# One explicit table for the order of 1435 operations, in place of a list scheduler, in a one-core attention and feed-forward kernel

## The chip, the core and the metric

The kernel runs on one core of one Trainium2 chip. That core has a matrix engine (TensorE, called PE below), a vector engine (DVE), a scalar engine (ACT), a general engine (POOL) and a synchronising engine (SP). Each runs its own instructions[...] and waits on semaphores for the others. Here POOL and SP mainly issue DMA transfers. The metric is the device time of one execution in microseconds, as the median of several runs, lower being better.

## What is computed

Eight batches of twelve heads go through an attention whose softmax is replaced by a squared ReLU. Its output, a matrix of 3584 rows and 768 columns, goes through a feed-forward block of width 2048 with an exact GELU.

```python
# batch 8, heads 12, sequence S = 448, head width 64
scores = scale * np.matmul(q, k.transpose(0, 1, 3, 2))
attn = np.maximum(scores, 0.0) ** 2 / S
x = np.matmul(attn, v)          # -> (3584, 768)
h = x @ w_in                    # 768 x 2048
g = 0.5 * h * (1.0 + erf(h * inv_sqrt2))
return g @ w_out                # 2048 x 768
```

## The kernel before

The kernel describes its work as 1435 objects of class `Op`. An `Op` is a short burst of work on one engine, such as four matmuls of one score tile, or one copy. It names the engines that may run it with assumed durations, the operations it depends on, and the buffers it takes and frees. A scheduler written in Python decides at build time the order on each engine and, where an `Op` may run on ACT or DVE, which of the two runs it. Nothing of the scheduler runs on the chip; only the order that it made does.

The operations fall into kinds. Letters in brackets are the `mode` of PE operations.

- Score tiles `fn_qk` [A]: four or eight matmuls with stationary tiles of 64 x 64, which use the four quarters of the array side by side, into a buffer `ps` out of three of the PSUM pool `w`. `fn_relu` (ACT or DVE) brings them to SBUF, `fn_mul` (DVE) squares them there.
- `pav` [A]: 28 matmuls of squared scores with values, also on quarters, once seven score tiles are squared. Two copies (ACT or DVE) bring them to `xT`.
- First feed-forward product [F]: `psh` for batches 0 to 4, and `pb` (one level of Strassen's method, with sums formed on DVE) for batches 5 to 7, on the whole array of 128 x 128. ACT applies GELU.
- Second product `pso` [F]: four plain products, then 13 groups of seven Strassen products each, into a buffer out of two of the PSUM pool `f`; copied or added into an output tile `osb`, of which there are three, and stored.
- Transposes on PE [T] for batches 0 and 1, `tp`. For batches 2 to 7 the transposes are done by DMA, issued from SP, and stores are issued from SP as well.
- `fill` [A]: matmuls of zeros early on, to keep PE busy.

```python
SWITCH = 0.09
PASSES = 5
...
ORDER = """
A10 P11 D13 A16 D12 P17 D18 P14 G0 P42 A15 G1 P39 A40 G2 P19 D43 ...   # 267 operations,
... Z1056 P69 ...               # Z: a fill of so many columns
"""
...
    def pick(self, ops, only=None):
        ...
                if eng == "PE" and op.mode != self.mode:
                    est += SWITCH
                key = (est + op.bias + x * op.other, n)
        ...

    def run(self, fixed):
        best = None
        for _ in range(PASSES):
            self.reset()
            self.place(fixed)
            self.deadlines()
            end = self.free["PE"]
            if best is None or end < best[0]:
                best = (end, list(self.log))
        self.open, self.log = [], best[1]

        def at(x):
            est, op, eng = x
            if eng not in ("ACT", "DVE"):
                return est
            return est + next(lat for e, _, lat in op.engines if e == eng)

        for est, op, eng in sorted(self.log, key=at):
            op.fn(eng)

    def place(self, fixed):
        ...
        for word in ORDER.split():          # first the table
            if word[0] == "Z":
                op, eng = next(fills), "PE"
            else:
                op, eng = self.open[int(word[1:])], names[word[0]]
            ...
            self.commit(max(self.ready(op), free), op, eng, dur, lat)
        ...
        while rest or any(fixed.values()):  # then the list scheduler
            ...                             # earliest estimated start first
```

The score tile, its evacuation and its square:

```python
            o1 = sch.add((("PE", d, d + 0.24),), fn_qk, deps, need=("w",), mode="A", bias=bias)
            d = 0.19 + 0.00069 * 2 * used
            eng = (("ACT", d, d + 0.14),)
            d = 0.07 + 2 * used / 960
            if dve:
                eng += (("DVE", d, d + 0.12),)
            o2 = sch.add(
                eng, fn_relu, [o1], need=("a",), frees=("w",), bias=bias, other=RELU_DVE
            )
            ...
            o3 = sch.add((("DVE", d, d + 0.12),), fn_mul, [o2], bias=bias)
```

A group of the second product. `v2` and `v3` take the two output tiles of the group; `p4` needs `v3`, and `p3` needs `c22`:

```python
        p1 = product("a", lambda: h(0, o1), lambda: quad[0, 0], done, need=("f",))
        v1 = passed("a", first, None, [p1], need=("p",))
        p6 = product("b", lambda: box["s", 2], lambda: tsum(2), done + sums + [s2], need=("f",), frees=("s2",))
        ...
        v2 = passed("b", part(0, right), first, [v1, p6], need=("osb",))
        p2 = product("a", lambda: h(1, o1), lambda: quad[1, 0], [v1])
        ...
        p7 = product("b", lambda: box["s", 3], lambda: tsum(3), [v2, s3], frees=("s3",))
        v3 = passed("b", part(1, right), first, [p7], need=("osb",))
        p5 = product("c", lambda: box["s", 1], lambda: tsum(1), [s1, s2], need=("f",), frees=("s1",))
        c22 = passed("c", part(1, right), part(1, right), [v3, p5])
        p4 = product("b", lambda: h(1, o2), lambda: tsum(4), [v3])
        ...
            sch.add((("SP", 0.6, 2.8),), store(1, full, [nc.sync] * 2), [c22, c21], frees=("osb",))
```

The DMA transposes are issued from SP, in the queue in which the stores stand; a small copy on POOL, the `gate`, waits for them and lets the loads of the next batch be issued:

```python
            return sch.add(
                (("SP", T_STEP, T_TIME),),
                lambda e: nc.sync.dma_start_transpose(dst(), src()),
                deps + old_T(b) + after.pop(0), mode="X",
            )
```

Of the kernel before, what the change touches and what calls it, by code (L numbers as in the profile page):

```python
# [47 lines left out]
RELU_DVE = 0.8  # L48
DMA_FREE = 3.05
DMA_LAT = 2.13  # L50
SWITCH = 0.09
LEAD = 8
HALF_M = 6
PASS_BIAS = -0.4
SUM_BIAS = -0.3
# [1 line left out]
LEADS = {}  # L57
SHARES = (1.3, 1.0, 1.0, 1.0, 1.0, 1.0)
LAST = 256
PASSES = 5  # L60
PULL = 0.15
PULL_IN = 0.45
NEAR = 0.25
# [17 lines left out]


ORDER = """
A10 P11 D13 A16 D12 P17 D18 P14 G0 P42 A15 G1 P39 A40 G2 P19 D43 G3 D44 P21 A22 P33 D20 P36 G4
Z128 P54 G5 P25 A37 P23 A55 G6 P51 D34 P48 A24 A49 D26 D35 D56 D41 D38 A52 Z1056 P69 D70 G7
Z1024 P57 Z992 P63 A58 D53 Z448 P45 D50 P66 G8 G9 D59 A64 A46 P27 P31 D28 G117 D32 A67 D65 D68
A47 G118 P60 P78 G119 A61 P29 D30 G120 P81 A79 A82 D62 G121 G122 Z1088 P93 A94 D71 P108 Z544
P84 A85 Z992 P75 D109 A76 D83 D80 P72 P90 D73 P129 D95 P105 A74 G123 P102 A91 D130 A106 P131
D86 D77 G124 D132 P141 D92 A103 P111 P96 G125 A112 P165 P143 A97 D104 P156 D107 A166 A157 P87
D113 D98 P99 D110 D88 G126 A142 D89 P114 P174 P133 D100 G127 A101 A175 D115 D116 P159 A144  # L90
P168 D134 G128 P171 D169 A160 P135 D172 D173 D170 A136 G147 P251 P192 D193 P186 P162 A252 P145
D176 A163 A146 P243 P253 P180 P195 A187 A244 P198 P137 A254 G148 D164 D158 P139 G149 G150 A181
D167 G151 A199 D161 P183 D196 A184 P177 D138 D140 D188 G152 P189 P219 P245 P247 D194 A178 A190
S231 A220 D185 A179 P207 P216 A246 S229 D182 P213 D191 D197 P261 A248 A208 S232 P263 S228 D200
A214 P222 D217 P204 D221 D209 P201 D215 A262 A223 A264 P210 A211 P265 G153 S230 A266 P259 A260
P249 P255 D218 D205 A202 A250 A203 P257 D224 G154 A256 D206 D212 P225 P267 G155 A258
"""


# [14 lines left out]
class Scheduler:  # L114
# [110 lines left out]
        self.open, self.log = [], best[1]  # L225


        def at(x):
            est, op, eng = x
            if eng not in ("ACT", "DVE"):  # L230
                return est
            return est + next(lat for e, _, lat in op.engines if e == eng)

        for est, op, eng in sorted(self.log, key=at):
            op.fn(eng)

    def deadlines(self):
# [97 lines left out]
def kernel(  # L335
# [119 lines left out]
    def e_copy(n, psum=4):  # L455
# [4 lines left out]
    sch = Scheduler({"w": 3, "a": NA, "f": 2, "osb": 3, "s1": 1, "s2": 1, "s3": 1, "s4": 1,  # L460
                     "p": 1})
# [384 lines left out]
    def add_wsums(after, done):  # L846

        last = [o[0] for (bb, *_), o in list(Tq.items()) + list(Tk.items()) if bb == B - 1]
        last += [o for (bb, *_), o in QK.items() if bb == B - 2]
        add, sub = mybir.AluOpType.add, mybir.AluOpType.subtract  # L850

        def one(n, m0, op, a, b, deps):
            m1 = m0 + M1 // 2
            return sch.add(
                (("DVE", 0.95, 1.07),),
                lambda e: V.tensor_tensor(wcols(n, m0, m1), a(m0, m1), b(m0, m1), op=op),
                deps + last + after,
            )

        def part(i, j):  # L860
            return lambda m0, m1: wpart(i, j, m0, m1)

        def summed(n):
            return lambda m0, m1: wcols(n, m0, m1)

        for m0 in (0, M1 // 2):
            s1 = one(1, m0, add, part(0, 1), part(1, 1), [])
            s2 = one(2, m0, sub, summed(1), part(0, 0), [s1])
            s4 = one(4, m0, sub, part(1, 0), summed(2), [s2])
            s3 = one(3, m0, sub, part(0, 0), part(0, 1), [s1] + done)  # L870
            WS[m0] = {1: s1, 2: s2, 3: s3, 4: s4}
# [48 lines left out]
    def add_block(b, m4, y, ms, bank, x, t, TS, xs, old, half):  # L920

        tmp = {}

        def product(name, left, right, deps, first=False):
            def fn(e):
                if first and name not in bank:
                    bank[name] = w_pp.tile([128, 2, NB], F32, tag="w", name="pb")
                for z, m in enumerate(ms):
                    w, mm = left(m)
                    for k in range(K1):  # L930
                        nc.tensor.matmul(  # L931
                            bank[name][:, y, z * HS : z * HS + HS],
                            w[:, k, bass.ts(mm, 128)],
                            right()[:, k],
                            start=first and k == 0 and z == 0,
                            stop=k == K1 - 1,
                            skip_group_check=not first or z > 0,
                        )

            d = 2 * K1 * (HS / 2400 + 0.0025)  # L940
            return sch.add(
                (("PE", d, d + 0.24),), fn, deps, mode="F",
                need=("w",) if first and y == 0 else (),
            )

        def plain(i, j):
            return lambda m: (wpart(i, j), m)

        def summed(n):
            return lambda m: wtile(n, m)  # L950

        def ps(name):
            return bank[name][:, y, :S]

        def get(name):
            if name not in tmp:
                tmp[name] = apool.tile([128, S], F32, tag="a", name="part")
            return tmp[name]

        def passed(name, to, other, deps, need=()):  # L960
            def fn(e):
                if other is None:
# [28 lines left out]
        c11 = gelu(lambda: ps("a"), 0, 0, [p2], ("w",))  # L991
        p7 = product("b", summed(3), t(3), [v2, W[3], TS[3]])
        v3 = passed("b", "u", "p", [p7], ("a",))
        p5 = product("c", summed(1), t(1), [W[1], TS[1]], True)
        c22 = passed("c", "u", "u", [v3, p5])
        g22 = gelu(lambda: get("u"), 1, 1, [c22], ("a",))
        p4 = product("b", plain(1, 1), t(4), [v3, TS[4]])
        c21 = passed("b", "p", "p", [p4, v3, v2])
        c21.frees = ("w",)
        g21 = gelu(lambda: get("p"), 1, 0, [c21], ("a",))  # L1000
        p3 = product("c", summed(4), x(1, 1), [c22, W[4]])
        c12 = passed("c", "t", "t", [p3])
        c12.frees = ("w",)
        g12 = gelu(lambda: get("t"), 0, 1, [c12], ("a",))
        for name, o in (("a", c11), ("b", c21), ("c", c12)):
            bank.setdefault(("end", name), []).append(o)
        return [p1, p6, p2, p7, p5, p4, p3]
# [25 lines left out]
    def add_tsums():  # L1033

        def sub(n, c, a, b, deps):
            return sch.add(
                (("DVE", 0.95, 1.07),),
                lambda e: V.tensor_sub(tsum(n)[:, c], a()[:, c], b()[:, c]), deps, bias=TSUM_BIAS,
            )

# [24 lines left out]
    def add_group(g):  # L1065
# [13 lines left out]
        def sum_op(n, op, a, b, deps):  # L1079
            def fn(e):  # L1080
# [1 line left out]
                V.tensor_tensor(box["s", n], a(), b(), op=op)  # L1082

            o = sch.add(
                (("DVE", 0.69, 0.8),), fn, deps, need=(f"s{n}",), bias=SUM_BIAS
            )
            mine.append(o)
            return o
# [200 lines left out]
    o = early("ACT", lambda: nq[0][:, :4, : HC * D], q32, 5.3)  # L1289
# [70 lines left out]
    for b in range(2, B):  # L1360
# [9 lines left out]
        if b + 1 < B:  # L1370

            n = {2: 2}.get(b, 1)
# [91 lines left out]
```

## Time and profile before

| | before |
|---|---|
| device time, median of 3 | 371.81 us (371.18 to 372.02) |
| span of the profiled execution | 369.5 us |
| busy time of PE, DVE, ACT | 361.4, 280.9, 204.8 us |
| mean granted PE clock | 0.997 |
| score tiles evacuated (L686 on ACT, L688 on DVE) | 139 and 30 |
| squares on DVE, L695 | 169, mean 616 ns |
| copies to `xT` on DVE, L451 | 45, mean 581 ns |

The page shows, for one execution, the busy time of each engine, the same in 40 slices of the span, the DMA queues, the chain of work that ended last, and the costliest groups of instructions with what ended the idle time before them. A start-to-start distance is the surest measure on PE, since matmuls overlap and the ends in the profile are modelled. In the timeline a row merges neighbouring instructions: its first number is the start of the first, its second the time to the end of the last. `PEld` is the loading of stationary tiles. A time in brackets at a row's end is idle time of the engine before it, with what ended it.

### The profile page before, as it was taken

The numbers are of one execution on the slowest core, as the hardware profiler recorded it, in microseconds if no ns is written. First come the engines' busy times: TensorE is split into PE (matmuls) and PEld (weight loads), VectorE is DVE, ScalarE is ACT, GpSimd is POOL, SyncE is SP. The second block draws the span as 40 slices with busy tenths as digits, with TensorE's granted clock in tenths as the row PEclk, the third lists the DMA queues.
The fourth block names the chain that finished last, engine by engine and source line by source line (L and its number), as shares of the span: only waits on it lengthen the run. The fifth ranks groups of instructions, "written<-read, shape, count | busy, mean of one in ns | idle before, by whom it ended". The sixth has DMA issues, their size and how long they took to land.

```text
span 369.5 us, 8514 instructions
## 1 busy us (share of the span) xinstructions
PE 361.4 (98%) x3573; PEld 222.9 (60%) x3573; DVE 280.9 (76%) x479; ACT 204.8 (55%) x313; POOL 63.5 (17%) x103
## 2 busy tenths in 40 slices
PE   8999999999999999999999999999999999999994
PEld 7675645455544455554455544447876897688663
DVE  3999930789887688997688979998778558765862
ACT  4998954755377745777764578853540353045200
POOL 8666304230112114040212000000000000000000
PEclk9999999999999999999999999999999999999998
DMA  9999999999999999999999992002002301210232
GB/s 174 195 202 204 202 185 167 194 202 171 159 217 208 163 163 204 189 167 162 180 169 117 164 200 64 2 1 87 2 0 87 88 0 46 87 40 2 85 87 85
DMA packets 89269, 47.27 MB, mean 128 GB/s; under 512 B 55312, under 2 KB 85776, under 8 KB 89232
## 3 DMA queue, kind: packets, MB, share of 16 engines
q0 software_dynamic: 32912, 22.47, 44.7%
q1 hardware_dynamic: 55952, 23.76, 36.6%
q8 instruction: 28, 0.46, 0.5%
q10 hardware_dynamic: 368, 0.51, 0.4%
q14 instruction: 9, 0.07, 0.1%
HBM read 45.61 MB, written 11.01 MB: 153 GB/s over the span
## 4 chain that ended last, share of the span: by engine, by line
PE 86%; DMA 3%; SPq 3%; DVE 2%; issue 1%; POOL 1%; ACT 1%; DVEq 0%; POOLq 0%; ACTq 0%
PE pso L1101 29%; PE psh L787 25%; PE pb L931 13%; PE ps L674 9%; PE pav L735 7%; SPq L600 3%; DMA nq<-in_q_dram 2%; PE pso L1196 1%; ACT a_sq L686 1%; DMA out_dram<-osb 1%; DVE osb L1135 1%; PE tp L573 1%; DVE part L965 1%; POOL v_sb L504 1%; PE tp L545 0%
## 5 line engine op out<-in xcount | busy, mean ns | idle before, releaser
L686 ACT ACTIVATE a_sq<-ps 128x896 bf16<-128x896 f32 x139 | 120.1, 921 | 32.0 <-PE ps L674 31.8
L695 DVE TENSOR_TENSOR a_sq<-a_sq 128x896 bf16<-128x896 bf16 (+1 forms) x169 | 98.2, 616 | 4.5 <-ACT a_sq L686 3.4
L787 PE MATMUL psh<-xT,win_sb 128*128 128x448 bf16 (+1 forms) x516 | 96.3, 340 | 0.0
L787 PEld LDWEIGHTS <-win_sb 128*128 128x128 bf16 x516 | 48.0, 98 | 45.1 <-issue 9.2
L797 ACT ACTIVATE h_sb<-psh 128x448 bf16<-128x448 f32 x80 | 43.8, 549 | 29.9 <-PE psh L787 29.9
L1101 PEld LDWEIGHTS <-s_sb 128*128 128x128 bf16 x424 | 40.4, 98 | 27.3 <-issue 3.2
L688 DVE TENSOR_SCALAR a_sq<-ps 128x896 bf16<-128x896 f32 (+1 forms) x30 | 32.1, 1073 | 24.8 <-PE ps L674 24.7
L965 DVE TENSOR_TENSOR part<-pb,part 128x448 f32<-128x448 f32 x60 | 34.6, 620 | 21.5 <-PE pb L931 21.5
L674 PE MATMUL ps<-qT,kT 64*64 64x448 bf16 (+1 forms) x756 | 48.6, 336 | 1.2 <-ACT a_sq L686 0.4
L1101 PEld LDWEIGHTS <-h_sb 128*128 128x128 bf16 x312 | 29.9, 98 | 21.8 <-issue 3.3
L1101 PE MATMUL pso<-wout_sb,s_sb 128*128 128x384 bf16 (+2 forms) x216 | 38.1, 320 | 0.1
L1101 PE MATMUL pso<-wout_sb,h_sb 128*128 128x384 bf16 x208 | 38.1, 326 | 0.0
L1101 PE MATMUL pso<-t_sb,s_sb 128*128 128x384 bf16 x208 | 38.1, 326 | 0.0
L735 PE MATMUL pav<-a_sq,v_sb 64*64 64x448 bf16 (+1 forms) x756 | 36.5, 329 | 0.0
L674 PEld LDWEIGHTS <-kT 64*64 64x64 bf16 x756 | 18.6, 105 | 24.7 <-issue 17.8
L974 ACT ACTIVATE h_sb<-part 128x448 bf16<-128x448 f32 x36 | 20.1, 578 | 20.2 <-DVE part L965 19.9
L451 DVE CAST xT<-pav 128x448 bf16<-128x448 f32 (+1 forms) x45 | 24.4, 581 | 7.9 <-PE pav L735 7.6
L1135 DVE TENSOR_TENSOR osb<-pso,p_sb 128x384 f32<-128x384 f32 x39 | 21.7, 556 | 9.8 <-PE pso L1101 5.3
L931 PEld LDWEIGHTS <-win_sb 128*128 128x128 bf16 x288 | 27.6, 98 | 2.3 <-issue 0.4
L735 PEld LDWEIGHTS <-v_sb 64*64 64x64 bf16 x756 | 21.0, 107 | 11.8 <-issue 1.6
L641 POOL COPY gate<-qT 128x16 bf16<-128x16 bf16 x15 | 4.3, 284 | 113.8 <-DMA qT<-nq 113.8
L931 PEld LDWEIGHTS <-ws 128*128 128x128 bf16 x216 | 20.7, 98 | 0.0
(61 smaller groups left out, 294.6 us busy)
## 6 DMA issues: line engine op xcount, KB each, us to landing
nk<-in_k_dram POOLq DMA_DIRECT2D x23, 224.0 KB, 6.7
nq<-in_q_dram POOLq DMA_DIRECT2D x21, 224.0 KB, 8.6
v_sb<-in_v_dram POOLq DMA_DIRECT2D x5, 672.0 KB, 15.0
out_dram<-osb SPq DMA_DIRECT2D x8, 336.0 KB, 3.0
v_sb<-in_v_dram POOLq DMA_DIRECT2D x9, 224.0 KB, 8.2
out_dram<-osb SPq DMA_DIRECT2D x7, 288.0 KB, 3.2
out_dram<-osb SPq DMA_DIRECT2D x8, 240.0 KB, 3.0
win_sb<-in_moe_w_in_dram POOLq DMA_DIRECT2D x8, 192.0 KB, 8.5
```

Of the source, the lines that this page charges most:

```text
L451: V.tensor_copy(dst, src)
L674: nc.tensor.matmul(ps[64 * j : 64 * j + 64, e, x * w : x * w + w], kT[r, g, i * 128 + 64 * j : i * 128 + 64 * j + 64], moving, start=True, ...
L686: A.activation(ar, ps, AF.Relu, scale=c_att)
L688: V.tensor_scalar(ar, ps, c_att, 0.0, op0=mybir.AluOpType.mult, op1=mybir.AluOpType.max,)
L695: V.tensor_mul(box["a2"][:, :, :used], ar, ar)
L735: nc.tensor.matmul(pav[0][o2 : o2 + 64, e, :w], vt[b][r, 2 * g + e, bass.ts(i, D)], box["a2"][r, y, o : o + w], start=(i == 0), stop=(i == ...
L787: nc.tensor.matmul(ph[:, x * n : x * n + n], win_sb[:, kd, bass.ts(m + x, 128)], xT[b][:, kd, c], start=(kd == 0), stop=(kd == KD - 1),)
L797: A.activation(h_ring()[:, m : m + nm, o + c.start : o + c.stop], box[0][:, :S].rearrange("p (x n) -> p x n", x=nm), AF.Gelu,)
L931: nc.tensor.matmul(bank[name][:, y, z * HS : z * HS + HS], w[:, k, bass.ts(mm, 128)], right()[:, k], start=first and k == 0 and z == 0, st ...
L965: V.tensor_add(get(to), ps(name), get(other))
L1101: nc.tensor.matmul(box[bank][:, n0:n1], left()[:, kf], right()[:, kf, n0:n1], start=bool(need) and kf == 0, stop=kf == K2 - 1, skip_group_ ...
L1135: V.tensor_add(out()[:, n0:n1], box[bank][:, n0:n1], other()[:, n0:n1])
```

## The change

The short table with the list scheduler behind it gives way to one table that names all 1435 operations, engine by engine, in one sequence. The table was made with changes of the array's division (between quarters and the whole array) charged at 0.11 us each instead of 0.09. The operations, tiles, buffers and arithmetic stay as they are. Apart from the table:

```diff
-SWITCH = 0.09
+SWITCH = 0.11
...
-PASSES = 5
+PASSES = 1
...
 ORDER = """
-A10 P11 D13 A16 D12 P17 D18 P14 G0 P42 A15 G1 P39 A40 G2 ...
-... (267 operations and the fills)
+G0 G1 G2 G3 G4 G5 G6 A10 P11 D13 A16 P17 G7 D12 P14 D18 P42 ...
+... S400 P326 P423 A331 D323 S386 A334 P342 A422 P336 P339 P425 D424 D329 A340 P427 D337 S402
+A343 D341 A426 G407 P429 D344 G408 S403 D428 G409 P431 D335 D332 S389 D560 P437 P440 D338 P345 ...
+... (1427 operations and the fills)
 """
...
-        def at(x):
-            est, op, eng = x
-            if eng not in ("ACT", "DVE"):
-                return est
-            return est + next(lat for e, _, lat in op.engines if e == eng)
-
-        for est, op, eng in sorted(self.log, key=at):
+        for _, op, eng in self.log:
             op.fn(eng)
...
-                (("DVE", 0.95, 1.07),),        # sums of weights, at two places
+                (("DVE", 0.86, 1.07),),
...
-                (("DVE", 0.69, 0.8),), fn, deps, need=(f"s{n}",), bias=SUM_BIAS
+                (("DVE", 0.6, 0.8),), fn, deps, need=(f"s{n}",), bias=SUM_BIAS
...
-            return sch.add(
-                (("PE", d, d + 0.24),), fn, deps, mode="F",
+            o = sch.add(
+                (("PE", d, d + 0.24),), fn, deps + bank.get(("first", name), []), mode="F",
                 need=("w",) if first and y == 0 else (),
             )
+            if first:
+                bank["first", name] = [o]
+            return o
```

The last part makes the product that opens a `pb` buffer come before the others that use it. In the table a letter gives the engine (P, A, D, G, S for PE, ACT, DVE, POOL, SP) and the number the operation; `D428` is `v3` of the first group of the second product, `P431` its `p4`, `S386` and `S389` the stores of the first two output tiles.

More of the change, by code (lines that the diff above doesn't have):

```diff
@@ L83 @@
 ORDER = """
[L84 to L95, printed above, removed]
@@ L96 @@
-P249 P255 D218 D205 A202 A250 A203 P257 D224 G154 A256 D206 D212 P225 P267 G155 A258
+G0 G1 G2 G3 G4 G5 G6 A10 P11 D13 A16 P17 G7 D12 P14 D18 P42 P39 G8 P19 A15 P21 D43 P33 P36 D44
+A40 D20 Z128 A22 P54 G9 P25 P23 A37 D34 P51 D26 P48 A55 Z1056 D35 A24 P69 D56 Z1024 D41 A49
+P57 Z992 D38 A52 P63 Z448 G117 D70 P45 A58 D53 P66 A64 D50 P27 A46 G118 P31 D59 P60 D28 A67
+G119 D32 A47 P78 P29 D65 G120 A61 P81 Z1088 D68 D30 A79 P93 D62 P108 Z544 D71 A82 P84 Z992
+G121 A94 P75 D109 P72 G122 D83 A85 P90 P129 D80 G123 D73 A76 P105 A74 P102 D95 G124 P131 D130
@@ new lines @@
+A91 P141 D86 A106 D77 P111 P96 D132 A103 P165 P143 D92 A112 D104 D107 A97 P156 D113 P87 G125
+D98 A166 P99 D110 G126 D88 A157 P114 A144 D100 A89 P159 G127 A101 P168 D167 P133 D115 A142
+P135 D116 G128 A160 P171 P174 D134 P251 A169 D136 A175 P162 D172 P195 P192 D170 P145 A252 D158
+A196 D176 P243 G147 D173 A146 G148 P253 D163 A193 D164 A244 P183 G149 P198 D161 P180 P139 A254
+G150 P137 D184 A181 P186 P177 G151 A140 D199 D138 P189 A187 P210 D197 P247 A178 D200 G152 D182
+G153 A190 P245 A179 D211 A248 G154 P207 P216 P222 P263 A246 G155 A208 D217 P265 D191 A264 D185
@@ new lines @@
+P261 D194 A223 D188 A266 P219 S231 P213 D212 P204 P255 A262 D220 S229 A214 P259 D224 D209 A256
+P249 S232 D215 A205 D221 P201 D218 D206 A250 P225 S228 A202 A260 P257 A203 S230 A226 P267 D227
+A258 P352 S234 A268 P348 S233 A353 P350 G237 A349 G238 S235 P276 P285 P282 P358 A351 G239 S236
+D277 P356 G240 G241 A359 P354 A286 P294 A283 P279 P291 A357 P362 A355 P360 D292 A363 D295 P366
+D287 A361 P300 P288 D280 P306 P364 A367 D284 P370 D289 A365 D307 P368 D296 A371 G242 P376 D301
+G269 D281 A369 P374 D290 G270 D278 A377 G271 P372 D293 G272 P324 G273 P297 A373 A375 P303 D325
@@ new lines @@
+P315 P382 D302 G274 A316 A298 D390 A299 P378 G275 D391 D304 P312 P318 P309 D383 P384 A379 D305
+A310 S398 D393 A319 D392 S399 P380 D394 A385 D317 S401 A313 D395 D417 P387 D311 D320 A381 D397
+D314 D308 P327 P321 D418 D419 A328 P333 P330 D420 P421 A322 A388 D396 S400 D326 P423 A331 D323
+S386 A334 P342 A422 P336 P339 P425 D424 D329 A340 P427 D337 S402 A343 D341 A426 G407 P429 D344
+G408 S403 D428 G409 P431 D335 D332 S389 D560 P437 P440 D338 P345 S404 D430 A438 P443 D441 P446
+S405 P433 D442 A346 D432 A347 P509 A444 D434 A447 P452 D439 G410 P449 P455 S406 D448 P511 G411
@@ new lines @@
+A510 D445 G412 A453 P513 S435 D456 S436 A512 P517 D450 D457 A514 P515 D451 D454 P464 D562 P461
+P458 S541 D561 A516 A465 P470 D462 P467 G413 S542 A518 P519 G414 G415 D471 A468 P521 S543 D463
+G416 A520 D472 P523 D459 S544 A522 D563 P473 A460 P476 D469 P479 P525 A524 A474 D477 P527 A480
+D478 A526 D466 P529 D481 A528 D475 P485 P488 P482 S545 A530 D486 A489 P491 P494 P531 D483 P533
+D492 D484 S546 A532 P535 D490 A495 D493 A534 P503 P497 P500 P537 A536 G550 G551 D504 S547 A501
+P564 G552 D502 A498 D496 S548 A538 P539 D487 G553 D499 P600 G554 P603 D505 P506 D565 G555 A540
@@ new lines @@
+S549 A601 P609 D604 P606 P566 D605 A507 A508 P568 A610 D567 P570 D607 D569 P618 D611 P615 P612
+P572 D571 S704 A619 D582 P574 A613 S705 D573 A616 P576 D580 G556 S706 D620 G557 D575 P624 G558
+P627 D602 S578 P633 P584 D617 G559 A625 D581 S707 D577 P586 A628 D614 A585 D608 S579 P639 D629
+A634 P630 G713 P621 G714 G715 A640 P636 D631 P642 S708 P588 D641 A622 D587 D635 A643 P590 A623
+D583 A589 D632 P592 D626 A637 D644 D591 P648 P651 D638 P645 S709 A649 P657 D652 P654 P594 D593
+D646 A655 D723 P596 A647 D656 D653 A658 S710 P663 D595 P660 P666 P672 D724 D597 A661 D659 P674
@@ new lines @@
+D650 A664 S711 A673 P676 D665 D662 A667 A675 P766 D668 P763 P669 S712 D725 A767 P769 D764 G716
+A677 P772 S598 P678 D768 G717 S599 D670 A770 G718 P680 G719 A679 P682 A773 G720 A671 D774 P775
+P781 A681 P778 G721 S867 D771 P684 A683 G722 D776 A779 P686 S868 D726 D765 A685 P688 D780 A782
+D777 A687 P790 D783 P787 P784 A791 S869 P793 D788 A689 P796 P690 D792 D789 A794 P692 A785 D795
+A691 P694 A797 A786 D798 P802 P805 A693 P799 P696 A695 S870 D803 A806 P698 D804 A800 A697 P700
+D801 D807 A699 P814 P811 P808 S871 A701 A815 P817 D812 P820 P702 D809 S872 A821 P727 D818 G876
@@ new lines @@
+D810 G877 A703 S873 P915 G878 P826 P823 P729 D728 D813 A916 S874 P731 A824 D827 G879 D730 G880
+D828 P909 S875 P921 P829 D819 G881 P733 D732 D825 A922 P735 D822 A830 D816 D831 A910 P906 P924
+D734 P832 D743 A925 P933 D907 P912 P737 D736 A934 P739 D935 A913 A833 D738 S741 P948 D744 P918
+P747 D917 G882 D740 G883 D926 A919 P749 S978 G884 A834 D745 A748 G885 D920 P972 S742 D914 A949
+P939 P945 D923 P751 D911 A973 S979 D750 P753 D908 A946 D950 A940 D752 P954 S980 P930 P927 D754
+A931 P936 D955 P942 P755 D941 D956 A937 D928 P757 A929 D756 A943 P957 D746 P969 P960 P759 D758
@@ new lines @@
+D938 A970 P837 S981 D971 A958 D760 P835 D932 A838 D886 P841 D974 A961 D947 A836 P843 D962 S982
+D944 A842 P839 D959 S983 A844 P963 P966 P951 S984 D964 A967 P987 P993 P847 D888 S985 A952 D965
+A840 D1067 P845 D953 S761 D1068 A848 P849 D968 S986 A994 A846 D988 P990 P999 P975 S762 D989
+A850 A1000 D991 P1002 P996 P851 D1001 A976 D1003 P853 A997 D1070 A977 D1004 A852 P855 D1059
+A854 D995 P1020 P1011 P1005 P857 A856 D1063 D992 A1021 P859 D998 A1006 D1007 P1026 A1012 P1014
+P1008 A858 D1060 A1027 D887 P1017 A860 D1022 P861 D1009 A1015 D1028 P863 A1018 D1013 A862
@@ new lines @@
+D1010 P1035 P1023 D1019 P1029 P865 A864 D1069 D889 A1024 P890 D1016 A1036 A866 P892 D1062
+D1037 A1030 A891 D1025 P894 D1031 D1061 P1041 P1038 P1032 D1066 D1064 A1039 P1044 D893 P896
+A895 D1033 A1042 D1034 P898 D1040 A1045 D1043 P1047 D897 P1050 P1053 D1046 P900 D899 A1048
+D1139 P902 A1051 D1049 D1140 A1054 P1071 D1052 D1055 P1056 D901 S904 A1072 D903 S905 P1088
+D1141 P1073 D1057 P1090 A1089 D1058 P1143 D1074 D1091 P1075 D1065 P1092 A1144 D1142 P1077
+A1076 D1179 P1094 A1093 D1180 P1079 D1078 P1096 D1095 P1145 D1080 D1097 A1081 P1082 D1181
@@ new lines @@
+A1098 P1099 D1146 P1085 D1083 P1102 D1100 P1147 D1086 D1293 P1105 D1103 P1107 P1122 A1106
+P1183 D1108 P1149 D1148 A1123 A1084 P1109 P1124 P1126 A1110 P1111 D1125 P1128 D1150 A1127
+P1151 A1184 D1112 D1291 D1182 P1113 D1129 P1200 D1292 P1116 D1114 P1133 A1201 P1130 A1104
+D1117 P1119 D1134 P1153 D1131 D1152 A1132 P1185 D1120 A1135 P1136 A1121 D1154 S1157 P1204
+A1101 D1186 A1087 P1202 D1137 P1191 A1138 P1189 A1118 D1203 P1206 A1115 P1155 D1190 D1207
+P1194 D1161 P1163 D1159 P1187 P1208 D1164 P1211 D1195 P1167 D1192 D1156 S1158 D1209 P1197
@@ new lines @@
+D1212 P1217 D1160 P1214 P1165 A1218 P1221 P1234 D1166 P1169 D1198 D1294 A1235 D1168 P1171
+D1215 D1162 P1219 D1170 P1236 D1253 P1173 D1172 D1251 P1238 D1252 P1175 D1237 D1220 P1223
+P1240 D1176 A1199 P1255 A1222 D1224 A1188 D1241 A1205 P1225 D1174 S1177 A1196 P1228 S1178
+A1216 P1242 A1239 D1226 P1245 D1256 P1259 D1229 D1246 P1295 D1243 P1231 P1257 A1296 A1213
+D1232 A1230 P1297 D1254 A1233 P1248 D1258 A1227 P1312 A1260 D1298 P1261 A1313 P1314 P1263
+D1262 D1249 P1301 D1315 A1250 P1318 A1210 A1193 P1265 D1302 A1247 D1264 A1244 P1267 D1319
@@ new lines @@
+D1271 D1266 S1269 P1303 D1272 P1323 D1273 P1275 D1268 S1270 D1304 P1320 P1277 A1276 D1321
+P1279 D1324 D1278 P1326 P1309 A1280 P1281 P1306 P1283 D1282 D1310 P1299 D1307 P1285 D1274
+D1284 D1327 P1329 D1363 P1287 D1286 S1289 A1330 D1364 P1346 D1365 P1331 A1300 D1366 P1316
+A1305 P1348 A1347 D1332 P1335 A1311 D1288 S1290 A1317 P1337 D1349 A1325 P1352 D1336 A1328
+P1354 A1308 D1338 P1340 D1353 A1339 P1343 A1322 D1355 P1357 D1341 A1356 P1360 D1344 A1342
+P1350 D1358 A1345 P1333 D1361 A1359 P1367 A1351 A1362 P1369 A1334 D1368 P1371 D1370 P1373
@@ L97 @@
+D1372 P1375 D1374 P1377 D1376 P1379 D1383 D1378 S1381 P1387 D1384 D1380 S1382 P1389 D1388
+P1391 D1385 D1386 D1390 P1393 D1392 P1395 D1394 P1397 D1405 D1396 P1399 D1403 D1398 S1401
+P1407 D1404 D1400 S1402 P1409 D1406 D1408 P1411 D1410 P1413 D1412 S1423 P1415 D1414 P1417
+D1416 P1419 D1418 S1424 P1420 D1421 S1425 D1422 S1426
 """
@@ L1036, in sub @@
             return sch.add(
-                (("DVE", 0.95, 1.07),),
+                (("DVE", 0.86, 1.07),),
                 lambda e: V.tensor_sub(tsum(n)[:, c], a()[:, c], b()[:, c]), deps, bias=TSUM_BIAS,
```

## The prediction, as put on record

> **What bounds the kernel now.** I read the page first: busy time, slices, chain.
>
> ```profile
> PE 361.4 (98%) x3573; PEld 222.9 (60%) x3573; DVE 280.9 (76%) x479; ACT 204.8 (55%) x313; POOL 63.5 (17%) x103
> ...
> PE   8999999999999999999999999999999999999994
> ...
> PEclk9999999999999999999999999999999999999998
> DMA  9999999999999999999999992002002301210232
> ...
> PE 86%; DMA 3%; SPq 3%; DVE 2%; issue 1%; POOL 1%; ACT 1%; DVEq 0%; POOLq 0%; ACTq 0%
> ```
>
> PE sets the end: 86% of the chain and every slice but the first and last. But the DMA engines are busy too until slice 24 (222 us), and 6% of the chain is DMA and SP's queue. So a gain of PE is a gain only where no transfer stands in its way.
>
> Busy is not useful, so I counted. In the chain, 80 matmuls of 384 columns take 13.00 us, 162.5 ns each, which is columns / 2.4 + 2.5 ns; a 448-column one takes 189.2 ns by the same form, and four quarter-array matmuls share that time. With the counts of the groups: whole array 267.9 us, the 45 opening matmuls 2.5, quarters 63.7, fills 2.7, transposes on PE 4.7; together 341.5. The first matmul starts at 1.0 us and the last at 364.6, so 22 us of 363.6 are neither. About 2 us of these are the opening matmuls at a slow clock. The rest are changes of array division, and waits. The timeline of PE in the steady part shows the changes:
>
> ```profile
> 106.98 0.76 PE L674 MATMUL ps<-qT,kT 64*64 64x448 bf16 x12
> 107.67 3.58 PE L787 MATMUL psh<-xT,win_sb 128*128 128x448 bf16 x18
> 111.18 0.57 PE L674 MATMUL ps<-qT,kT 64*64 64x448 bf16 x8
> ```
>
> From 106.98 to 107.67 twelve quarter-array matmuls (12 x 189.2 / 4 = 0.568 us) take 0.69: 0.12 too much. From 107.67 to 111.18 eighteen whole ones (3.405) take 3.51: 0.105 too much. One change costs about 0.114 us. In the built order of the kernel before I count 119 changes, 13.6 us.
>
> For the waits I looked for starts later than the matmuls before them explain. After the opening 27 us they are few: 0.50 us at 31.89 and about 0.2 at 28.04 and 29.13; 0.45 at 99.39; 0.3 each at 102.99 and 192.78 (a row of eight score matmuls is 0.86 or 0.87 us long instead of 0.55); 0.62 at 244.54; 0.24 at 276.56. That is all there is to win besides changes. The one at 99.39 differs in kind. The chain from 76 to 104 us has
>
> ```profile
> 94.93 0.53 SPq L1062
> ...
> 95.52 3.17 DMA out_dram<-osb
> ...
> 98.78 0.56 DVE osb L1135
> ```
>
> and the timeline
>
> ```profile
> 84.91 6.86 SPq L600 DMA_TRANSPOSE kT<-nk  x1
> 91.87 2.97 SPq L600 DMA_TRANSPOSE qT<-nq  x1
> 94.93 1.00 SPq L1062 DMA_DIRECT2D out_dram<-osb  x2
> ...
> 97.64 1.46 PE L1101 MATMUL pso<-t_sb,s_sb 128*128 128x384 bf16 x8
> ...
> 98.78 0.56 DVE L1135 TENSOR_TENSOR osb<-pso,p_sb 128x384 f32<-128x384 f32 x1 [0.96 <-DMA out_dram<-osb]
> ...
> 99.39 1.46 PE L1101 MATMUL pso<-t_sb,h_sb 128*128 128x384 bf16 x8 [0.29 <-DVE osb L1135]
> ```
>
> The first store stands in SP's queue behind four DMA transposes. It lands at 98.7 us, only then is an output tile free for `v3`, and only then can `p4` run: `p5` began at 97.64, its eight matmuls take 1.30 us, so PE could have gone on at 98.94 and did at 99.39.
>
> **What the Trainium skill says.** "TensorEngine Tiling (Array Packing)", Key Properties: changing the tiling mode drains the TensorE. The trace agrees, 0.105 and 0.12 us a change. "TensorE: Matmul & The Clock Gate", Back-to-back issue gap: columns / 2.4 + 2.5 ns for the single gap; the 162.5 ns above are exactly that. The same page, Architectural detail: ScalarE and VectorE are strict first in, first out. The trace fits, the `v3` addition holding DVE idle for 0.96 us at 98.78; what stands behind it in the table waits with it. "Trainium Kernel Development and Optimization", Key Constraints: transfers from the SP, ACT and POOL queues run on the same 16 DMA engines. The slices near full until 222 us fit.
>
> **The change, part by part**, from the built order of both programs.
>
> Unchanged: the orders on POOL and on SP are identical, so loads, transposes and stores are issued in the same sequence; the matmuls are the same 3573; the first 52 PE operations (to about 25 us) and the last 18 are in the same order.
>
> Changes of division: 119 become 110. Three of the nine lie before `p4` at 99.39, six after. Worth 9 x 0.114 = 1.0 us in all, 0.34 and 0.68.
>
> Engines: 26 evacuations of score tiles go from ACT to DVE and nine back, net 17; 22 copies to `xT` go from DVE to ACT. DVE: 17 x 1.073 - 22 x 0.581 = +5.5 us of busy time, ACT: about -3, taking 0.92 and about 0.55 us. DVE is then some 286 us of 369, 78%: no bound, but less air in a strict queue.
>
> Up to 99.39: I expect no gain to survive. The transposes ahead of the store began at 82.16, when the loads for them had landed. These loads are the same, on DMA engines that are full. So the store should land at 98.7 again, within half a microsecond. What the new order gains before that (0.34 of changes, up to 0.9 of waits) makes PE arrive earlier at `p4` and wait longer. Gain 0. Moreover the table puts `D335` and `D332` behind `D428`, which is the held addition; before, they stood ahead of it. `D338` follows too. They are squares that the `pav` after two more score tiles needs at once. From 98.78: 0.47 for the addition, two squares of 0.58, a sum of 0.60, a square of 0.6 gives about 101.7, and before, that `pav` started at 101.18. It can use the first squares a little earlier, so I charge 0.3 us.
>
> After 99.39: six changes, -0.68. Waits of 0.3, 0.62 and 0.24 can go, 1.16 in all. The one at 244.54 I believe in: there ACT stood with four score evacuations behind an `osb` copy that waited for its product, and the new order puts evacuations ahead of such copies. For the rest I take half of the sum, -0.6, since new orders bring new waits: the last 110 us, which had almost none, are reshuffled, with five places where a product follows 1.15 us after its evacuated predecessor (the least was 1.30).
>
> Sum: 371.8 - 0.68 - 0.6 + 0.3 = 370.8 us.
>
> **Rivals.** (a) All is kept: the anchor at 98.7 us moves along with PE, or PE has enough other work there. Then -1.0 for changes and up to -2 for waits, 368.8 to 369.5. For it: the group's score tiles stand earlier in the new order. Against: SP's order is unchanged and its transposes wait for loads, not for PE. (b) The table trades waits for changes: in the strict queues squares and evacuations stand behind operations that are held, and PE waits at many places for 0.1 to 0.5 us. Ten such waits give back 2 to 3 us, 372 to 373.5. For it: DVE gets busier and the order is tight everywhere. Against: the gaps between a score tile and the reuse of its buffer are hardly shorter (the least after 99 us is 1.52 in both orders). (c) A load or a DMA transpose comes late, since score tiles of batches 2, 6 and 7 stand 3 to 15 us earlier in PE's order. Each such wait could be several microseconds, 374 or more. Against: the transposes of batch 7 are issued by 219.6 us and its last score tiles start at about 234 in the new order, those of batch 6 have some 5 us.
>
> **Range and chances.** The middle lies between (a) and (b), with my sum nearer to (a). Eight times in ten I expect 369.2 to 372.5: the lower end is (a), the upper a mild (b). Two per cent are 7.4 us; there are no 7 us of waits and spared changes to win, and only (c) could lose so much. Chances: faster by over 2% 0.02, within 2% 0.95, slower 0.03.
>
> **What would show it.** Right: in the timeline of PE the run-to-run excess stays at 0.105 and 0.12 us; the store lands near 98.7 and `p4` starts at 99.2 to 99.8, after a wait of 0.8 to 1.5 us in place of 0.45; `pav` after it starts 0.2 to 0.5 us later than 101.18; from there to the end PE is 1.0 to 1.6 us shorter; no wait at 244. Wrong: `p4` before 99, or a wait of over 0.7 us elsewhere, above all one ended by a DMA or in the last 110 us.

## The result, and the profile after

| | before | after |
|---|---|---|
| device time, median | 371.91 us (371.02 to 373.54, 6 runs) | 376.89 us (376.20 to 378.37, 6 runs) |
| after / before | | 1.0136, 95% interval 1.0107 to 1.0165 |
| span of the profiled execution | 369.5 us | 374.7 us |
| changes of division on PE | 119 | 110 |
| score tiles evacuated on ACT, on DVE | 139, 30 | 122, 47 |

The kernel became 5 us slower. The page of the kernel after, in the lines that answer to those shown of before:

```profile
PE 361.2 (96%) x3573; PEld 222.5 (59%) x3573; DVE 284.3 (76%) x477; ACT 197.7 (53%) x315; POOL 64.0 (17%) x103
...
PE   7999999999999999999999999999998999989995
...
PEclk9999999999999999999999999999999999999998
DMA  9999999999999999999999980011011030211232
...
PE 93%; DVE 3%; DMA 1%; POOL 1%; issue 1%; ACT 0%; DVEq 0%; POOLq 0%
```

PE is as busy as before, the clock is the same, and DMA and SP's queue have all but left the chain. What is new is an 8 in slice 31 and another in slice 36 of PE's row (281 to 290 and 328 to 337 us), where the DMA engines are nearly idle, and DVE with 3% of the chain.

How much was lost where can be had from the starts of the matmuls alone. I took each start-to-start distance on PE, less the time of the matmuls between (columns / 2.4 + 2.5 ns; a quarter of it for matmuls on quarters, half of it for the transposes), and put what is left under "change" where the division changes and under "wait" elsewhere. Up to 27 us both kernels have the same order on PE, and "wait" also holds the 45 opening matmuls there, most of which come 107 ns apart in place of 55.8.

| stretch | change, before | change, after | wait, before | wait, after |
|---|---|---|---|---|
| 0 to 27 us | 2.61 | 3.42 | 5.03 | 4.68 |
| 27 to 100 us | 3.36 | 2.96 | 1.59 | 1.73 |
| 100 to 260 us | 6.97 | 6.29 | 2.43 | 1.47 |
| from 260 us | 0 | 0 | 0.23 | 6.97 |

The differences add up to +5.3 us, against 5.2 us between the spans. The middle of the kernel gained 1.64 us, as was hoped; the last 110 us lost 6.7. There are eleven waits there: 0.95 us at 269.77 (ahead of operation 1128), 0.95 at 280.79 (1206), 1.11 at 288.77 (1197), 0.77 at 305.39 (1259, a `pso` product), 0.95 at 315.56 (1318), 0.95 at 335.76 (1335), and five of 0.15 to 0.37 after 337. All but 1259 are products into `pb`. The profile's list of waits names who ended most of them; its numbers are the total in us, the times and the longest:

```profile
PE pb L993 <- DVE part L1030: 4.3, 6, 0.9
```

The timeline around the first of them:

```profile
266.52 0.74 PE L993 MATMUL pb<-xT,win_sb 128*128 128x224 bf16 x6
...
267.10 0.74 PE L993 MATMUL pb<-xs,ws 128*128 128x224 bf16 x6
...
267.67 0.74 PE L993 MATMUL pb<-xT,win_sb 128*128 128x224 bf16 x6
268.25 0.74 PE L993 MATMUL pb<-xs,win_sb 128*128 128x224 bf16 x6
...
269.09 0.62 DVE L1030 TENSOR_TENSOR part<-pb,part 128x448 f32<-128x448 f32 x1 [2.59 <-PE pb L993]
...
269.77 0.73 PE L993 MATMUL pb<-xs,win_sb 128*128 128x224 bf16 x6 [0.79 <-DVE part L1030]
```

The DVE addition at 269.09 reads the product that began at 267.10, and the product at 269.77 needs the addition. The first of these products began its last matmul at 267.58, and DVE had been idle for 2.59 us. Yet the addition began only 0.36 us after the last matmul of 268.25, two products later. What it waited for is the question of the experiments.

### The profile page after: what moved, and what is told of

Its sections match the earlier page's. It is cut to its first block, busy times and chain, and to the rows that moved or that the text cites. A ratio compares the mean times of both kernels' runs of the same rounds, so it can differ in the third digit from the quotient of the medians.

```text
span 374.7 us, 8467 instructions
## 1 busy us (share of the span) xinstructions
PE 361.2 (96%) x3573; PEld 222.5 (59%) x3573; DVE 284.3 (76%) x477; ACT 197.7 (53%) x315; POOL 64.0 (17%) x103
## 4 chain that ended last, share of the span: by engine, by line
PE 93%; DVE 3%; DMA 1%; POOL 1%; issue 1%; ACT 0%; DVEq 0%; POOLq 0%
PE pso L1166 32%; PE psh L849 25%; PE pb L993 13%; PE ps L736 10%; PE pav L797 9%; PE pso L1261 3%; DVE part L1030 2%; DMA nq<-in_q_dram 1%; PE tp L635 1%; DVE a_sq L757 1%; POOL nk L548 0%; PE tp L607 0%; PE fill L1493 0%; DVE a_sq L750 0%; DVE osb L1200 0%
## 5 line engine op out<-in xcount | busy, mean ns | idle before, releaser
L748 ACT ACTIVATE a_sq<-ps 128x896 bf16<-128x896 f32 (+1 forms) x122 | 107.3, 918 | 35.6 <-PE ps L736 35.5
L750 DVE TENSOR_SCALAR a_sq<-ps 128x896 bf16<-128x896 f32 (+1 forms) x47 | 50.3, 1077 | 20.2 <-PE ps L736 20.2
L1030 DVE TENSOR_TENSOR part<-pb,part 128x448 f32<-128x448 f32 x60 | 35.8, 620 | 20.1 <-PE pb L993 15.8
L515 ACT COPY part<-pb 128x448 f32<-128x448 f32 x12 | 6.3, 533 | 37.2 <-PE pb L993 37.2
L1039 ACT ACTIVATE h_sb<-part 128x448 bf16<-128x448 f32 x36 | 18.9, 571 | 9.6 <-DVE part L1030 9.4
```

Of the source, the lines that this page charges most:

```text
L748: A.activation(ar, ps, AF.Relu, scale=c_att)
L750: V.tensor_scalar(ar, ps, c_att, 0.0, op0=mybir.AluOpType.mult, op1=mybir.AluOpType.max,)
L1039: A.activation(h_ring()[:, m : m + 2, o + half[c].start : o + half[c].stop], src().rearrange("p (x n) -> p x n", x=2), AF.Gelu,)
```

## What a `pb` buffer is

The part of the kernel that the first section left out:

```python
for y in range(2):                      # two halves: rows ms of the product
    todo.append(add_block(b, m4, y, ms, bank, ...))
...
def product(name, left, right, deps, first=False):
    def fn(e):
        if first and name not in bank:  # one tile for both halves
            bank[name] = w_pp.tile([128, 2, NB], F32, tag="w", name="pb")
        for z, m in enumerate(ms):
            ...
            nc.tensor.matmul(bank[name][:, y, z * HS : z * HS + HS], ...)
...
p6 = product("b", summed(2), t(2), [W[2], TS[2]], True)
v2 = passed("b", "t", "p", [v1, p6], ("a",))       # DVE: part <- pb + part
p7 = product("b", summed(3), t(3), [v2, W[3], TS[3]])   # adds to the same buffer
```

Each half `y` has `NB` = 512 f32 values a partition to itself (a bank, in the expectations below), and neither half needs the other's data. A "drain" below is a DVE addition such as `v2`, which takes a product out of the buffer. "Emission" is the order of the whole list, over all engines, in which the instructions are written into the program. In all profiles read here the matmuls, and the instructions of DVE, start in the program's order; between engines it is the semaphores that hold one back for another. In the stretch shown, P1124 is `p6` of half 1 (267.10), D1125 its `v2` (269.09), P1128 its `p7` (269.77), and P1111 is `p7` of half 0 (268.25). In the new table these stand as `P1124 P1126 A1110 P1111 D1125 P1128`: P1111 is emitted ahead of D1125. The semaphore waits in the built program say that D1125 waits for P1111, not for P1124: dependencies are kept for the whole tile, in the order of emission, so an addition for one half waits for every product into the tile that was emitted before it. The kernel before has such waits too, and they cost nothing there: in its built program 30 of the 60 additions wait for the other half's product, but that product is always the very next one on PE. In the new program only 25 wait for the other half, but for 13 of them 12 matmuls or more lie between their own product's end and the end of the one that they wait for.

The theory: the table interleaves the halves, and emission order turns this into false waits. Rivals: the addition is late on DVE for another reason in the new order (other work, the moved evacuations); or the loss stems from the first 250 us, whose gain shifts work into a collision later.

## The experiments

None leaves out any of the work. Kernels of one comparison ran beside the kernel before on the same chip (371.28 us for the first four, 371.6 for the others).

**The new table up to 250 us, the old order after it.** The first 345 PE operations and what goes with them are the new table's.

```diff
  ... D1058 P1143 D1074 D1091 P1075 D1065 P1092 A1144     # new table to here
- D1142 P1077 A1076 D1179 P1094 A1093 ...
+ P1077 D1142 A1076 D1179 P1094 A1093 ...                 # order of before
```

> The new table up to 250 us (its first 345 PE operations with what stands before them), then the order of the kernel before. Theory (the new order gains in the first 250 us, and loses in the Strassen blocks of the last 110 us because the two halves of a pb buffer count as one tile): PE stays 1.4 us ahead of the kernel before to the end, 370.4 us, no wait over 0.2 us after 256 us. Rival (the loss comes from what the first part leaves behind, such as sums formed late or a fuller DVE): the waits after 265 us stay, 375 to 377 us.

Measured (the hybrid, below): 370.02 us, ratio to before 0.9964 (0.9952 to 0.9976). From 260 us on 0.23 us of waits are left, as in the kernel before. The gain of the first part stays; the loss belongs to the order after 250 us.

**The reverse: the old order up to 250 us, the new table after it.**

> The order of the kernel before up to 250 us, then the new table. Theory: all of the loss and none of the gain, 371.8 + 6.7 = 378.5 us, with the same four waits of 0.95 us. Rival (loss from the first part): 371.8 us.

Measured: 378.68 us, 1.0193 (1.0176 to 1.0210), with the same waits of 0.95, 0.95, 1.10, 0.77, 0.95 and 0.95 us. The old first part gives the late order the same waits, so the rival by way of the first 250 us falls. (One wait of 1.2 us at 154.7 came on top: an addition had been held for 2.36 us by a store that landed late, as told below under the stores.)

**Emission alone: the new table, six additions emitted earlier.** The sequence on every engine stays; only the place of six DVE operations relative to PE's in the list changes.

```diff
- P1124 P1126 A1110 P1111 D1125 P1128
+ P1124 P1126 A1110 D1125 P1111 P1128
  # likewise D1203 P1189, D1315 P1301, D1332 P1348, D1195 P1211, D1226 P1242
```

> The new table with the sequence on each engine unchanged; only six drains of pb (D1125, D1203, D1315, D1332, D1195, D1226) are emitted a few words earlier, ahead of the PE product of the other half that they waited for. Theory (waits are set per tile in the order of emission): the drains start right after their own product; the PE product of the other half waits for them instead, 0.37 us in place of 0.95 at four places; 1.1 and 0.4 us more at the other two: 376.9 - 3.8 = 373.1 us. Rival (the sequence on the engines or a too short drain time is the cause): the sequences are the same, so 376.9 us.

Measured: 373.01 us, 1.0057 (1.0032 to 1.0081). Its PE timeline, at the same place:

```profile
267.51 0.74 PE L991 MATMUL pb<-xT,win_sb 128*128 128x224 bf16 x6
268.46 1.31 PE L991 MATMUL pb<-xs,win_sb 128*128 128x224 bf16 x12 [0.21 <-DVE part L1028]
```

P1111 and P1128 now run back to back (x12), and the wait has moved ahead of P1111 and shrunk from 0.95 to 0.37 us: now P1111, emitted after D1125, waits for it, which it need not either. From 260 us on 2.98 us of waits are left of 6.97. So no operation's place on its engine was at fault here; the order of emission was.

**The dose: the old order, six additions emitted later.** The reverse edit in the kernel before, again with every engine's sequence unchanged.

```diff
- ... D1108 D1125 P1109 P1126 A1148 P1111 A1110 P1128
+ ... D1108 P1109 P1126 P1111 D1125 A1148 A1110 P1128
  # likewise D1091 P1077, D1203 P1189, D1237 P1223, D1315 P1301, D1349 P1335
```

> The kernel before with the sequence on each engine unchanged; at six places, one per Strassen block of four column tiles, the drain of p6 of the second half is emitted after p7 of the first half. Theory: each such drain starts 0.95 us late and p7 of the second half waits for it, 6 x 0.95 = 5.7, 377.5 us. Rival (emission order costs nothing where the engines' sequences are the same): 371.8 us.

Measured: 377.44 us, 1.0155 (1.0139 to 1.0170). The first of the six places:

```profile
257.73 0.74 PE L991 MATMUL pb<-xs,win_sb 128*128 128x224 bf16 x6
...
258.58 0.62 DVE L1028 TENSOR_TENSOR part<-pb,part 128x448 f32<-128x448 f32 x1 [2.40 <-PE pb L991]
...
259.25 0.73 PE L991 MATMUL pb<-xs,win_sb 128*128 128x224 bf16 x6 [0.78 <-DVE part L1028]
```

It is the picture of the kernel after, made in the kernel before: six waits of 0.95 us, one of 0.47 at 262.75, and a loss of 6.2 us against the 6.7 of the new table's last part, without one operation changing its place on its engine.

**Two tiles in place of one.** So far emission was moved; this leaves the new table wholly alone and takes away what ties the halves. Once the last score tile has its buffer, two of the three `pb` buffers become two tiles of one bank each.

```diff
-                    bank[name] = w_pp.tile([128, 2, NB], F32, tag="w", name="pb")
+                    bank[name], bank["hold", name] = two_tiles(name)
...
+    def two_tiles(name):
+        i = free.pop(0)
+
+        if ring["n"] or i == BASE:      # the third buffer stays as it is
+            t = pools[i].tile([128, 2, NB], F32, tag="w", name="pb")
+        else:
...
+            t = tuple(
+                pools[i, "y"].tile([128, NB], F32, tag=f"y{x}", name=f"pb{x}") for x in range(2)
+            )
+        return t, [i, 2]
```

The edit also hands out the three buffers of the pool `w` from a list of free ones. Up to 260 us this shows in no wait on PE, but for one of 1.26 us at 206.36 that a late store causes (told at the end).

> The new table, its order unchanged on every engine and in emission. Once the last score tile has its buffer, two of the three pb buffers are each made of two tiles of one bank in place of one tile of two. In the built program v2 of D1125, D1203 and D1332, and D1195 and D1226, then wait for their own product; D1315 stays in the third, undivided buffer and waits for P1301 as before. If the two halves held each other through the common tile: the waits before 1128, 1206, 1197, 1259 and 1335 (0.95, 0.95, 1.11, 0.77, 0.95) go, 1318 keeps its 0.95, so some 4.7 us less than the new kernel, up to 5.8 if the small waits after 1335 go too: 371.1 to 372.2 us. If the waits came from DVE being late in this order for another reason, the buffers change nothing: 376.9.

Measured: 370.31 us, 0.9978 (0.9962 to 0.9994): 1.3 us below the kernel before in place of 5.0 above it. At the same place as above:

```profile
267.59 0.74 PE L1041 MATMUL pb<-xs,ws 128*128 128x224 bf16 x6
...
268.16 0.74 PE L1041 MATMUL pb<-xT,win_sb 128*128 128x224 bf16 x6
268.43 0.62 DVE L1078 TENSOR_TENSOR part<-pb,part 128x448 f32<-128x448 f32 x1 [1.44 <-PE pb L1041]
268.74 1.31 PE L1041 MATMUL pb<-xs,win_sb 128*128 128x224 bf16 x12
```

The addition starts 0.36 us after the last matmul of its own product (267.59 + 5 x 0.096 = 268.07), and P1111 and P1128 follow without a gap. From 260 us on 0.98 us of waits remain, 0.95 of them in the undivided buffer:

```profile
310.66 0.74 PE L1041 MATMUL pb<-xs,win_sb 128*128 128x224 bf16 x6
311.51 0.62 DVE L1078 TENSOR_TENSOR part<-pb,part 128x448 f32<-128x448 f32 x1 [1.43 <-PE pb L1041]
312.19 0.73 PE L1041 MATMUL pb<-xs,win_sb 128*128 128x224 bf16 x6 [0.78 <-DVE part L1078]
```

One kernel thus holds both: divided buffers without the wait, the undivided with it. More went than I had put down: 6.0 us by this profile, since the waits of 0.15 to 0.37 us after 337 went too. The common tile is the cause.

**Two tiles, and the addition of the undivided buffer emitted earlier.**

```diff
- P1301 D1315
+ D1315 P1301
```

> As with the divided buffers, and in addition D1315 is emitted before P1301, which it stands behind in the table; every engine's own sequence is unchanged. If the common tile is the cause: the wait before 1318 falls from 0.95 to 0.37 (P1301 now waits for D1315), so 0.6 us below the kernel with divided buffers alone, 370.5 to 371.6 us. Otherwise no change from it.

Measured: 369.73 us, 0.9954 (0.9939 to 0.9969). The wait did not shrink to 0.37 but went altogether: here a `pso` product stands between P1314 and P1301, so the addition is done before P1301 is due. The timeline:

```profile
308.20 0.74 PE L1041 MATMUL pb<-xs,ws 128*128 128x224 bf16 x6
308.78 1.46 PE L1215 MATMUL pso<-t_sb,s_sb 128*128 128x384 bf16 x8
310.07 1.31 PE L1041 MATMUL pb<-xs,win_sb 128*128 128x224 bf16 x12
```

From 260 us to the end 0.04 us of waits are left. It has the lowest ratio of all, 0.5% below the kernel before and by the two ratios (0.9954 / 1.0136) 1.8% below the one after, though its interval overlaps with the hybrid's: the new order does what it was meant to once its buffers let it.

**The store ahead of two transposes.** A test of the prediction's other main point, in the kernel before: S386, the first store, leaves SP's queue ahead of the transposes S401 and S400.

```diff
- ... S401 ... S400 ... P387 D395 A385 S386
+ ... P387 D395 A385 S386 S401 S400
```

> The kernel before, with one change in SP's queue: the first output store ahead of two of the four DMA transposes. Anchor theory: the store lands near 91 us instead of 98.7, v3 of the first group waits for nothing, p4 starts 0.45 us earlier and all after it: 371.3 - 0.45 = 370.8 us. Rival (the wait at 99.39 is made up later, or the delayed transposes cost as much): 371.3 us or more.

Measured: 371.13 us, 0.9990 (0.9975 to 1.0004), an interval that holds 1. In its profile:

```profile
87.44 1.34 SPq L1125 DMA_DIRECT2D out_dram<-osb  x2
...
97.84 0.56 DVE L1198 TENSOR_TENSOR osb<-pso,p_sb 128x384 f32<-128x384 f32 x1
...
98.94 1.30 PE L1164 MATMUL pso<-t_sb,h_sb 128*128 128x384 bf16 x7
```

The store is issued at 87.44 in place of 94.93, `v3` no longer stands waiting, and `p4` starts at 98.94, 0.45 us earlier, exactly the wait. The wait of 0.29 us at 102.99 is gone as well, and the 0.75 us of both last to the end of this execution (244.54 has become 243.79). The medians, 371.13 and 371.62, differ by 0.49 us, but by the interval the gain isn't shown.

**Two early waits moved, in the hybrid; and that together with the early store.** P243, a `psh` product at 31 us, goes ahead of three score tiles, and two sums late in the kernel go behind an addition and another sum.

> The hybrid (new table to 250 us, order of before after it) with two of its waits taken out by the order alone: a feed-forward product of six pairs moved ahead of three score tiles at 31 us (wait 0.74 us there), and two sums on DVE moved behind the square sum that a product at 274 us waits for (0.23 us). If the first store, which stands behind four DMA transposes, anchors PE at 99 us, as predicted, only about 0.3 of the 0.74 survives: 370.0 - 0.3 - 0.2 = 369.5 us. If there is no such anchor: 370.0 - 0.95 = 369.1 us.

Measured: 370.71 us, 0.9965 (0.9950 to 0.9980), the hybrid's ratio, and neither of the two times expected. A few executions, the profiled one here (941.9 us) among them, were in a slow state; medians hold them, ratios don't, and that profile is not read.

> The previous two changes together on the hybrid: both waits taken out and the first store ahead of two transposes. Anchor theory: the whole 0.95 us of the two waits counts, 369.1 us, 0.4 less than with the store behind. Rival: as without the store's move.

Measured: 370.50 us, 0.9973 (0.9952 to 0.9993), not the 369.1 expected. The profile shows why. Both waits only moved (0.61 us at 32.03, 0.24 at 277.40), and at 152 us a late store holds an output tile once more:

```profile
136.10 8.33 SPq L660 DMA_TRANSPOSE qT<-nq  x2
144.52 1.74 SPq L1125 DMA_DIRECT2D out_dram<-osb  x2
146.36 2.06 SPq L660 DMA_TRANSPOSE kT<-nk  x1
...
152.39 0.56 DVE L1198 TENSOR_TENSOR osb<-pso,p_sb 128x384 f32<-128x384 f32 x1 [2.13 <-DMA out_dram<-osb]
...
152.86 0.61 DVE L755 TENSOR_TENSOR a_sq<-a_sq 128x896 bf16<-128x896 bf16 x1
...
153.53 1.33 PE L795 MATMUL pav<-a_sq,v_sb 64*64 64x448 bf16 x23 [1.57 <-DVE a_sq L755]
```

The store's data were ready at 143.2; it left SP's queue behind two transposes at 144.52 and landed 7.15 us after it had set out, at 152.27. An addition waits 2.13 us on DVE for its output tile, the square behind it waits too, and PE waits for the square. These two runs show no gain over the hybrid alone.

## Why the prediction was right and where it failed

Predicted were 370.8 us, 369.2 to 372.5; measured 376.89, above the range.

- *A change costs 0.114 us, six fewer after 99 us are worth 0.68.* Right: in the table of stretches 6.97 becomes 6.29. By this count one change costs a little less, 0.100 us before (70 changes) and 0.098 after (64), so that the sum fits this well is in part luck. The cost of a change, which the prediction tied to "TensorEngine Tiling (Array Packing)", Key Properties, is there in the new order too.
- *The first store anchors PE at 99.4, no gain survives before it.* The number came out, but by luck. `v3` began at 98.97, held by the store, and `p4` at 99.58, inside the 99.2 to 99.8:

```profile
98.08 1.46 PE L1166 MATMUL pso<-t_sb,s_sb 128*128 128x384 bf16 x8
...
98.97 0.56 DVE L1200 TENSOR_TENSOR osb<-pso,p_sb 128x384 f32<-128x384 f32 x1 [0.84 <-DMA out_dram<-osb]
...
99.58 1.46 PE L1166 MATMUL pso<-t_sb,h_sb 128*128 128x384 bf16 x8
```

The wait was 0.20, not 0.8 to 1.5 us, for PE did not come early: `p5` began at 98.08 in place of 97.64. The first 27 us, with the same order in both kernels, took 0.45 us more in this execution (their excess is 7.6 to 8.2 us over ten profiles). From 27 to 100 us the spared changes gave 0.40 us, as foreseen, but waits other than that of `p4` rose from 1.14 to 1.53 and took it back. Nor does the store hold PE in every execution. Where it stands behind the four transposes the profiles show:

| kernel | `p5` begins | `v3` begins | `p4` begins | wait before `p4` |
|---|---|---|---|---|
| before | 97.64 | 98.78 | 99.39 | 0.45 |
| after | 98.08 | 98.97 | 99.58 | 0.20 |
| dose | 98.04 | 99.34 | 99.95 | 0.61 |
| two tiles, addition moved | 97.63 | 98.88 | 99.49 | 0.56 |
| hybrid | 97.78 | 98.23 | 99.08 | none |
| two tiles | 97.86 | 98.18 | 99.16 | none |
| reverse | 98.22 | 98.42 | 99.52 | none |
| emission alone | 98.17 | 98.37 | 99.47 | none |

In the first four the store sets `p4`. In the last four it had landed by 98.4, and `p4` follows `p5` without a gap. So it hangs on the execution whether a gain ahead of `p4` survives, in the new order too.

- *`pav` behind it 0.3 us later.* 101.18 became 101.37, +0.19, just under the 0.2 to 0.5 named.
- *The wait at 244 goes.* Right. The matmuls that were at 244.54 are at 243.12, four score matmuls without a gap:

```profile
242.74 0.55 PE L797 MATMUL pav<-a_sq,v_sb 64*64 64x448 bf16 x8
243.12 0.36 PE L736 MATMUL ps<-qT,kT 64*64 64x448 bf16 x4
243.41 1.47 PE L1166 MATMUL pso<-wout_sb,s_sb 128*128 128x384 bf16 x8
```

- *"For the rest I take half of the sum, -0.6, since new orders bring new waits: the last 110 us, which had almost none, are reshuffled, with five places where a product follows 1.15 us after its evacuated predecessor (the least was 1.30)."* This is the step that failed. From 100 to 260 us the waits fell by 0.96, more than the 0.6. In the last 110 us, which the step names, they rose by 6.7. I measured the room between a product and its own predecessor, and by that measure the order was sound: from the end of a product to the next one that needs its addition PE takes 0.95 us when nothing lies between (268.82 to 269.77), and 1.15 is more. But the program waits by tile and by emission. P1128 stood 1.15 us after P1124, its true predecessor, and 0 us after P1111, the one that its addition was made to wait for. The count has to be made on the semaphore waits of the built program, which were there to be read before any run.
- *Rivals.* (b) foresaw 0.1 to 0.5 us at ten places on account of busy strict queues, (c) a late load or DMA transpose of several microseconds. The sum came out at (c)'s size, but the waits that brought it are ended by DVE, with DVE idle ahead of them, and not by a DMA. DVE's busy time rose by 3.4 us (5.5 were predicted) and ACT's fell by 7.1 (about 3); neither decided anything, since the last version has the same moves and the lowest ratio. (a), 368.8 to 369.5, is close to what the new order gives once the halves are apart, 369.73.

## What to carry to other kernels

When an order is rewritten by hand or by a table, the place in the list counts even between engines: of a product into a tile and an addition that reads the tile, the later emitted waits for the earlier, needed or not. Give parts that live separate lives separate tiles, or keep their accesses next to each other, and compare the semaphore waits of both built programs, not the planned distances. Their number says little (here it fell while the loss came); what counts is how much work lies between what an operation needs and what it waits for. A gain ahead of a transfer that may land late can become a wait; see from several profiles when it lands before counting the gain.

## What the runs showed beside that

- The chain product, DVE addition, next product costs the same wherever nothing lies between: 0.36 us from the start of the last matmul to that of the addition, 0.62 for the addition, and 0.95 us of idle PE from the end of the product (0.946 to 0.949 at all six places of the dose).
- The wait of 0.3 us at 103 us comes with the held `p4`: it is there in the four profiles with a wait before `p4` and in none of the others, nor in the two with the early store.
- That a late store holds an output tile is not tied to 99 us. It held DVE at 152 us for 2.13 us in one kernel, and in the profile of the kernel with two tiles at 204.75 us for 1.93, with 1.26 us lost on PE. That store was issued at 195.98, as soon as its data were there, and took 8.23 us to land; from 260 us on, after the last transpose, stores take 2.6 us in the median there. Whether the transposes or the loads beside it make a store slow wasn't tested.

```profile
204.75 0.56 DVE L1249 TENSOR_TENSOR osb<-pso,p_sb 128x384 f32<-128x384 f32 x1 [1.93 <-DMA out_dram<-osb]
...
206.36 0.38 PE L776 MATMUL ps<-qT,kT 64*64 64x448 bf16 x4 [1.09 <-DVE a_sq L790]
```

- The hybrid and the kernel with two tiles scatter more than the kernel before beside them: 368.81 to 372.21 us against 370.85 to 372.62, and 369.87 to 372.67 against 371.08 to 371.95. The last version does not in its four executions (369.37 to 369.85). That late stores in some executions are the reason is likely from these places, but wasn't tested by itself.
